# Four units of a retention layer transposed by DMA transfers instead of on TensorE, and the last output tile in two halves

## The chip, the cores and the metric

One NeuronCore of one Trainium2 chip. The metric is the device time of one execution in microseconds (us). Several executions are timed; one of them was also taken by the hardware profiler, and its trace is what the views below show. PE is TensorE (PEld its weight loads), DVE is VectorE, ACT ScalarE, POOL GpSimd, SP SyncE; SPq and ACTq are the parts of SP and ACT that issue DMA transfers.

## The reference

A recurrent retention layer over 4 batches, 8 heads, 768 steps and a head size of 64, followed by a feed-forward network over its 3072 tokens of width 512, with 2048 inner features:

```python
for t in range(S):
    state = gamma[None, :, None, None] * state + np.einsum('bhd,bhe->bhde', k[:, :, t], v[:, :, t])
    y[:, :, t] = scale * np.einsum('bhd,bhde->bhe', q[:, :, t], state)
...
x = attn_out.transpose(0, 2, 1, 3).reshape(B * S, H * D)
h = x @ w_in
g = np.maximum(h, 0.0) + alpha * np.minimum(h, 0.0)
out = g @ w_out
```

Inputs and output are float32; the kernel's matmuls take float16.

## The kernel before, in words

The recurrence is cut into chunks of 128 steps. A *unit* is two neighbouring chunks (256 steps) of four heads; there are 24 units, and four of them (512 tokens, all heads) make one of six *blocks*, on which the feed-forward network runs. The work on unit i:

- `load` (line 110) brings k, q and v of the unit, 256 KB each, on SP's queue, into tiles of a pool of 24 buffers that they share with the float32 pieces of w_out.
- `u_scale(i, 0)` multiplies k by its decay factors, on DVE, or on POOL where it is told so; `u_scale(i, 1)` does q on POOL (line 136). Both write one half of the tile kdq. `u_cast` (line 146) casts v to float16 (tile vx), on POOL (line 152) or ScalarE (line 150).
- kdq has to be transposed into the tile kq. `u_turn` (line 160) does it with eight PE transposes into PSUM (tile trb, line 166) and a copy on ScalarE (line 175). `u_flip` (line 154) does it with one DMA transfer that transposes, on SP's queue (line 156).
- `u_state` (tile stp, line 195) and `u_scores` (tiles sca and scb, line 236) are PE work; the scores read kq. DVE then masks the scores (line 249) and adds to the running state (lines 214, 218), and POOL decays it (line 219). `u_visit` (line 529) puts the state and the scores of one unit together.
- `u_out` (line 259 and after) multiplies masked scores with v and the carried state with q on PE (tile yps, lines 286 and 271), and ScalarE copies the result into xT (line 306), the input of the feed-forward network.

For each block n, `ffn1(n)` makes 16 groups of four matmuls (tile hps, line 326), each followed by a step on ScalarE (line 336) and one on DVE (gt, line 337); `ffn2(n)` multiplies gt with w_out, 64 matmuls into four PSUM tiles (tile ops, line 367), each copied by ScalarE (line 376) and stored. Both are generators: `tick(gen, m)` emits the next m matmuls, and the program writes work on the units between ticks, so that PE gets it between matmuls of the feed-forward network.

The order on every engine is the order of the program's text. Units 0 to 3 come first (0 to 22 us), with `u_turn`. Then `ffn1(0)` and `ffn2(0)` run; in `ffn2(0)` the work on units 4 to 7 is emitted, with `u_turn` as well. For blocks from 2 on, units are prepared on POOL and transposed by `u_flip` in `ffn1(n)`, and visited in `ffn2(n)`.

`ffn2(0)` runs in four parts (`parts=4`): all four output tiles first take w_out pieces 0 to 3, then 4 to 7 and so on, since the pieces are still being loaded and cast (`cast_wo`, on POOL at line 437 or on ScalarE at line 433). SP's queue, in its order: the loads of units 0 to 3, then w_out pieces 0 to 3, unit 4, pieces 4 to 7, unit 5, pieces 8 to 11, unit 6, pieces 12 to 15, unit 7, then units 8 to 11, four output stores, and from then on one `u_flip` ahead of each unit's loads. A transfer that has to wait for a semaphore holds up all that stand behind it on its queue. The transfers use eight completion semaphores in turn, and each waits for the one that had its semaphore before.

Of the kernel before, what the change touches and what calls it, by code (L numbers as in the profile page):

```python
# [9 lines left out]
FP = mybir.dt.float32  # L10
F16 = mybir.dt.float16
COPY = mybir.ActivationFunctionType.Copy
# [6 lines left out]
def kernel(  # L19
# [10 lines left out]
    nc = tc.nc  # L30
    B, H, S, D = q.shape
    d_model, d_ff = moe_w_in.shape
    NFT = d_ff // 128
# [4 lines left out]
    UB = 4  # L38
    NBLK = NU // UB
    TB = UB * C  # L40
    scale = 1.0 / np.sqrt(D)
# [30 lines left out]
    sbp = ctx.enter_context(tc.tile_pool(name="sbp", bufs=1, space=bass.MemoryType.SB))  # L72
# [13 lines left out]
    w_out_all = sbp.tile([128, NFT, d_model], F16, tag="wout", name="wout")  # L86
# [6 lines left out]
    def ps(name, dt=FP, n=512):  # L93
        return psp.tile([128, n], dt, tag="ps", bufs=8, name=name)
# [15 lines left out]
    def load(u, names="kqv"):  # L110
        t = staged.setdefault(u, {})
        for nm in names:
            src = srcs[nm]
            st = sbp.tile([128, H * D], FP, tag="ld", bufs=24, name=f"{nm}s{u}")
            j, g = divmod(u, 2)
            b, c = divmod(2 * j, NCH)
            t[nm] = st
            ins = nc.sync.dma_start(  # L118
                out=st.rearrange("p (h x) -> p h x", h=H // 2),
                in_=src[  # L120
                    b, H // 2 * g : H // 2 * g + H // 2, C * c : C * c + 2 * C, :
                ].rearrange("h (p s) d -> p h (s d)", s=2),
            )
# [4 lines left out]
    def u_scale(i, a, eng=None):  # L128
        if i not in prepped:
            kdq = sbp.tile([128, 2, 2, H // 2, D], F16, tag="kdq", bufs=8, name=f"kdq{i}")  # L130
            kq = sbp.tile([128, 2 * NP, 128], F16, tag="kq", bufs=8, name=f"kq{i}")
            vx = sbp.tile([128, H // 2, 2, D], F16, tag="vx", bufs=8, name=f"vx{i}")
            prepped[i] = (kdq, kq, vx)
        g = i % 2
        o = 2 * H * a
        (eng or (nc.vector, nc.gpsimd)[a]).tensor_tensor(  # L136
            out=prepped[i][0][:, a],
            in0=staged[i]["kq"[a]].rearrange("p (h s d) -> p s h d", s=2, d=D),
            in1=tab[:, o : o + 2 * H]
            .rearrange("p (s h) -> p s h", s=2)[:, :, H // 2 * g : H // 2 * g + H // 2]  # L140
            .unsqueeze(3)
            .to_broadcast([128, 2, H // 2, D]),
            op=MULT,
        )

    def u_cast(i, on_scalar=False):
        o = prepped[i][2].rearrange("p h s d -> p (h s d)")
        x = staged[i]["v"]
        if on_scalar:
            nc.scalar.activation(out=o, in_=x, func=COPY, bias=0.0, scale=1.0)  # L150
        else:
            nc.gpsimd.tensor_copy(out=o, in_=x)  # L152

    def u_flip(i):
        kdu, kq, vx = prepped[i]
        nc.sync.dma_start_transpose(
            out=kq, in_=kdu.rearrange("p a s h d -> p (a s h d)")
        )

    def u_turn(i, parts):  # L160
        kdu, kq, vx = prepped[i]
        trb = ps("trb", F16, 1024)
        for a in parts:
            for x in range(NP):
                c0 = 128 * (NP * a + x)
                nc.tensor.transpose(  # L166
                    out=trb[:, c0 : c0 + 128],
                    in_=kdu[:, a, x // 2, 2 * (x % 2) : 2 * (x % 2) + 2, :].rearrange(
                        "p a d -> p (a d)"
                    ),  # L170
                    identity=ident,
                )
        c0 = 512 * parts[0]
        c1 = 512 * parts[-1] + 512
        nc.scalar.activation(  # L175
            out=kq.rearrange("p a i -> p (a i)")[:, c0:c1],
            in_=trb[:, c0:c1],
            func=COPY,
            bias=0.0,
            scale=1.0,  # L180
        )
# [176 lines left out]
    def ffn2(n, parts=1, late=None):  # L358
        gt = gts.pop(n)
        opss = {}  # L360
        step = NFT // parts
        for f0 in range(0, NFT, step):
            for tq in range(UB):
                if f0 == 0:
                    opss[tq] = ps("ops")
                for ft in range(f0, f0 + step):
                    nc.tensor.matmul(  # L367
                        out=opss[tq],
                        lhsT=gt[:, ft, 128 * tq : 128 * tq + 128],
                        rhs=w_out_all[:, ft, :],  # L370
                        start=(ft == 0),
                        stop=(ft == NFT - 1),
                    )
                    if ft == NFT - 1:
                        os_sb = sbp.tile([128, d_model], FP, tag="os", bufs=6, name="os")
                        nc.scalar.activation(  # L376
                            out=os_sb, in_=opss[tq], func=COPY, bias=0.0, scale=1.0
                        )
                        row = TB * n + 128 * tq
                        if late is None:  # L380
                            nc.scalar.dma_start(out=out[row : row + 128, :], in_=os_sb)
                        else:
                            late.append((row, os_sb))
                    yield

    def tick(gen, m):
        for _ in range(m):
            if next(gen, 1) == 1:
                return
# [11 lines left out]
    for lh in range(2):  # L401
        z = slice(64 * lh, 64 * lh + 64)
        nc.gpsimd.tensor_copy(
            out=gmat[z, :, z],
            in_=tab[z, 4 * H : 4 * H + NP].unsqueeze(2).to_broadcast([64, NP, 64]),
# [9 lines left out]
    def hold(ins):  # L415
        if held:
            tc.add_manual_dep(
                ins.ins,
                held.pop().ins.name,
                mybir.DependencyInfo(  # L420
                    mybir.DependencyClass.Sync, mybir.DependencyReason.DATA
                ),
                reason="loads behind the pieces of w_in",
            )

    def load_wo(i):
        for ft in range(4 * i, 4 * i + 4):
            pieces[ft] = sbp.tile([128, d_model], FP, tag="ld", bufs=24, name=f"wo{ft}")
            hold(nc.sync.dma_start(out=pieces[ft], in_=moe_w_out[128 * ft : 128 * ft + 128, :]))

    def cast_wo(ft, on_scalar=False):
        if on_scalar:
            nc.scalar.activation(
                out=w_out_all[:, ft, :], in_=pieces.pop(ft), func=COPY, bias=0.0, scale=1.0
            )
        else:
            nc.gpsimd.tensor_copy(out=w_out_all[:, ft, :], in_=pieces.pop(ft))  # L437
# [4 lines left out]
    def masked(i):  # L442
        m[i](0)
        m[i](1)
# [53 lines left out]
    st[2](1)  # L498
    m[3](1)
    st[3](1)  # L500
    for i in range(UB):
        load_wo(i)
        load(UB + i)
    gen = ffn1(0, early=4)
    tick(gen, 8)
    u_out(2)
# [2 lines left out]
        out=aps[:, 0:NFT], in_=alpha_sb, identity=tab[0:NFT, NTAB - 16 : NTAB]  # L509
    )  # L510
    nc.vector.tensor_scalar(
        out=oma_sb, in0=aps[:, 0:NFT], scalar1=-1.0, scalar2=1.0, op0=MULT, op1=ADD
# [6 lines left out]
    u_cast(4)  # L519
    for ft in range(4, 8):  # L520
        cast_wo(ft)
    tick(gen, 52)
    u_scale(4, 0)
    for _ in gen:
        pass
    stores = []
    gen = ffn2(0, parts=4, late=stores)

    def u_visit(i):
        st[i] = u_state(i)  # L530
        m[i] = u_scores(i)
        st[i](0)
        masked(i)
        st[i](1)

    def u_prep(i, eng=None):
        u_scale(i, 0, eng)
        u_scale(i, 1)
        u_cast(i)

    tick(gen, 4)
    u_turn(4, (0, 1))
    tick(gen, 6)
    u_visit(4)
    u_prep(5)
    cast_wo(8)
    cast_wo(10)
    tick(gen, 10)
    u_out(4)
    tick(gen, 2)  # L550
    u_turn(5, (0, 1))
    cast_wo(9, True)
    cast_wo(11, True)
    tick(gen, 6)
    u_visit(5)
    u_prep(6)
    cast_wo(12)
    cast_wo(14)
    tick(gen, 8)
    u_out(5)  # L560
    tick(gen, 2)
    u_turn(6, (0, 1))
    cast_wo(13, True)
    cast_wo(15, True)
    u_scale(7, 1)
    u_cast(7)
    tick(gen, 6)
    u_visit(6)
    u_scale(7, 0)
    tick(gen, 8)  # L570
    u_out(6)
    tick(gen, 2)
    u_turn(7, (0, 1))
    tick(gen, 6)
    u_visit(7)
    for _ in gen:
# [5 lines left out]
    gen = ffn1(1, early=4)  # L582
# [3 lines left out]
    for n in range(1, NBLK):  # L586
        more = n + 1 < NBLK
        u0 = UB * (n + 1)
        if n > 1:
            gen = ffn1(n)  # L590
# [9 lines left out]
        gen = ffn2(n)  # L600
# [41 lines left out]
```

## Time and profile before

| | us |
|---|---|
| median of 3 runs (lowest, highest) | 217.64 (216.75, 220.69) |
| the profiled execution | 217.12 |
| its span, first to last instruction | 215.3 |
| units 0 to 3, until the first matmul of ffn1(0) | 0 to 17.4 |
| ffn1(0) | 17.4 to 33.6 |
| ffn2(0), with units 4 to 7 | 33.6 to 53.8 |
| last matmul ends | 211.5 |

A line of the chain of work, or of the timeline, has the start in us, the duration in us (of a merged group: from its first start to its last end, or its share of the chain), the engine, the tiles, the line of the kernel and the number of instructions. Some lines end in brackets with the idle time of the engine ahead of the instruction and what ended it. For a tile, three numbers such as 2.7/4.2/6.4 are minimum, median and maximum. The granted clock of PE is 0.998 of full speed in this execution.

### The profile page before, as it was taken

How to read it: one execution, taken by the hardware profiler on the slowest of the kernel's cores; microseconds unless marked ns; L12 is line 12 of the kernel's file. 1: busy time of each engine (PE TensorE's matmuls, PEld its weight loads, DVE VectorE, ACT ScalarE, POOL GpSimd, SP SyncE). 2: the span in 40 equal slices, each digit the busy share in tenths (PEclk: the TensorE clock that was granted, in tenths of full speed). 3: DMA queues.
4: the chain of work that ended last, by engine and by line, in shares of the span. 5: the costliest groups of instructions: out<-in, count | busy, mean ns of one | idle time of the engine just before them, and what ended most of it. 6: DMA issues, size and time to landing. Idle time of an engine off the chain costs nothing.

```text
span 215.3 us, 5025 instructions
## 1 busy us (share of the span) xinstructions
PE 207.2 (96%) x2053; PEld 105.4 (49%) x2053; DVE 120.6 (56%) x195; ACT 102.9 (48%) x189; POOL 87.0 (40%) x114
## 2 busy tenths in 40 slices
PE   7897999999999999999999999999999999999992
PEld 3455545555644555444555444555444555444440
DVE  2684697455398633488733488533488633488000
ACT  2582874556586223566223576223675223575121
POOL 3485084691891426930145960214950421000000
PEclk9999999999999999999999999999999999999999
DMA  6999999999699911899311799411840111100121
GB/s 168 317 223 200 279 368 373 369 336 331 222 208 313 277 61 49 221 242 307 110 52 52 194 241 298 148 53 49 139 108 0 49 52 52 49 0 2 52 81 65
DMA packets 62599, 36.11 MB, mean 168 GB/s; under 512 B 18912, under 2 KB 57456, under 8 KB 62576
## 3 DMA queue, kind: packets, MB, share of 16 engines
q1 hardware_dynamic: 57792, 28.32, 48.5%
q10 hardware_dynamic: 3200, 5.38, 6.9%
q0 software_dynamic: 1584, 2.10, 5.8%
q8 instruction: 16, 0.26, 0.5%
q14 instruction: 7, 0.06, 0.1%
HBM read 27.40 MB, written 6.29 MB: 156 GB/s over the span
## 4 chain that ended last, share of the span: by engine, by line
PE 89%; DMA 6%; SPq 2%; ACT 1%; POOL 0%; issue 0%
PE ops L367 40%; PE hps L326 39%; PE yps L286 4%; DMA win<-in_moe_w_in_dram 3%; DMA qs<-in_q_dram 3%; PE stp L195 2%; PE yps L271 2%; PE sca L236 2%; SPq L118 2%; PE trb L166 1%; ACT xT L306 1%; PE scb L236 1%; POOL kdq L136 0%; ACT os L376 0%
## 5 line engine op out<-in xcount | busy, mean ns | idle before, releaser
L337 DVE SCALAR_TENSOR_TENSOR gt<-hm,oma,hps 128x512 f16<-128x512 f32 x96 | 69.5, 746 | 35.6 <-ACT hm L336 28.4
L367 PE MATMUL ops<-wout,gt 128*128 128x512 f16 x384 | 89.2, 380 | 0.0
L326 PE MATMUL hps<-xT,win 128*128 128x512 f16 (+1 forms) x416 | 84.8, 363 | 1.2 <-ACT xT L306 0.7
L336 ACT ACTIVATE hm<-hps 128x512 f32<-128x512 f32 x96 | 56.6, 597 | 24.2 <-PE hps L326 23.6
L326 PEld LDWEIGHTS <-win 128*128 128x128 f16 x416 | 40.4, 98 | 43.8 <-issue 1.0
L219 POOL TENSOR_TENSOR tg<-ss,gmat 128x256 f16<-128x256 f32 x32 | 23.5, 735 | 78.2 <-DVE ss L218 72.7
L367 PEld LDWEIGHTS <-gt 128*128 128x128 f16 x384 | 35.3, 98 | 40.2
L306 ACT ACTIVATE xT<-yps 128x256 f16<-128x256 f32 x48 | 18.4, 453 | 40.8 <-PE yps L286 29.0
L376 ACT ACTIVATE os<-ops 128x512 f32<-128x512 f32 x24 | 14.2, 597 | 35.7 <-PE ops L367 35.7
L136 POOL TENSOR_TENSOR kdq<-qs,tab 128x512 f16<-128x512 f32 x24 | 25.0, 1044 | 5.4 <-DMA qs<-in_q_dram 5.4
L218 DVE TENSOR_TENSOR ss<-tg,stp 128x256 f32<-128x256 f16 x32 | 13.2, 416 | 24.3 <-PE stp L195 24.3
L249 DVE TENSOR_TENSOR m<-sca,mi 128x512 f16<-128x512 f32 x24 | 16.4, 685 | 0.8 <-PE sca L236 0.4
L136 POOL TENSOR_TENSOR kdq<-ks,tab 128x512 f16<-128x512 f32 x16 | 16.7, 1044 | 0.0
L249 DVE TENSOR_TENSOR m<-scb,mi 128x512 f16<-128x512 f32 x24 | 16.4, 681 | 0.0
L152 POOL CAST vx<-vs 128x512 f16<-128x512 f32 x20 | 13.2, 658 | 0.0
L175 ACT ACTIVATE kq<-trb 128x512 f16<-128x512 f16 (+1 forms) x11 | 8.7, 790 | 6.2 <-PE trb L166 6.2
L195 PE MATMUL stp<-vx,kdq 64*64 64x128 f16 x320 | 9.7, 219 | 0.7 <-ACT vx L150 0.7
L437 POOL CAST wout<-wo 128x512 f16<-128x512 f32 x12 | 7.5, 651 | 7.0 <-DMA wo<-in_moe_w_out_dram 6.9
L286 PE MATMUL yps<-m,vx 64*64 64x128 f16 x384 | 10.0, 222 | 0.0
L236 PE MATMUL sca<-kq 64*64 64x128 f16 x192 | 9.4, 216 | 0.5 <-ACT kq L175 0.4
L214 DVE TENSOR_TENSOR tg<-stp,gmat 128x256 f16<-128x256 f32 x8 | 3.4, 424 | 11.3 <-PE stp L195 11.3
L236 PE MATMUL scb<-kq 64*64 64x128 f16 x192 | 9.7, 219 | 0.0
(26 smaller groups left out, 73.4 us busy)
## 6 DMA issues: line engine op xcount, KB each, us to landing
ks<-in_k_dram SPq DMA_DIRECT2D x24, 256.0 KB, 4.5
qs<-in_q_dram SPq DMA_DIRECT2D x24, 256.0 KB, 4.7
vs<-in_v_dram SPq DMA_DIRECT2D x24, 256.0 KB, 4.5
out_dram<-os ACTq DMA_DIRECT2D x20, 256.0 KB, 2.0
wo<-in_moe_w_out_dram SPq DMA_DIRECT2D x16, 256.0 KB, 5.2
win<-in_moe_w_in_dram POOLq DMA_DIRECT2D x2, 768.0 KB, 8.8
out_dram<-os SPq DMA_DIRECT2D x4, 256.0 KB, 4.3
win<-in_moe_w_in_dram POOLq DMA_DIRECT2D x1, 512.0 KB, 6.4
```

The lines of the kernel that those rows point to most:

```text
L136: (eng or (nc.vector, nc.gpsimd)[a]).tensor_tensor(out=prepped[i][0][:, a], in0=staged[i]["kq"[a]].rearrange("p (h s d) -> p s h d", s=2, ...
L195: nc.tensor.matmul(out=stps[hf][64 * lh : 64 * lh + 64, 128 * r : 128 * r + 128], lhsT=kdu[z, 0, s, 2 * r + lh, :], rhs=vx[z, 2 * r : 2 * ...
L219: nc.gpsimd.tensor_tensor(out=tgs[u + 1][:, gs, :], in0=new, in1=gmat[:, gs, :], op=MULT)
L236: nc.tensor.matmul(out=scs[lh][z, c0 : c0 + 128], lhsT=kqv[y, 0, s, r, z], rhs=kqv[y, 1, :, r, z], start=True, stop=True,)
L249: nc.vector.tensor_tensor(out=m2, in0=scs[lh].rearrange("p (s r i) -> p s r i", s=2, r=2), in1=masku.unsqueeze(2).to_broadcast([128, 2, 2, ...
L286: nc.tensor.matmul(out=ypss[hf][64 * lh : 64 * lh + 64, 128 * r : 128 * r + 128], lhsT=vx[z, 2 * r + lh, s, :], rhs=m2s[lh][z, s, r, :], s ...
L306: nc.scalar.activation(out=xT[n][:, 2 * g : 2 * g + 2, c0 : c0 + C].rearrange("p a (i s) -> p a s i", s=2), in_=ypss[hf][:, 0:256].rearran ...
L326: nc.tensor.matmul(out=hpss[ft][:, lo:hi], lhsT=w_in_all[:, hp, 128 * ft : 128 * ft + 128], rhs=xT[n][:, hp, lo:hi], start=(hp == 0), stop ...
L336: nc.scalar.activation(out=hm, in_=hpt, func=RELU, bias=0.0, scale=-1.0)
L337: nc.vector.scalar_tensor_tensor(out=gt[:, ft, :], in0=hm, scalar=oma_sb[:, ft : ft + 1], in1=hpt, op0=MULT, op1=ADD,)
L367: nc.tensor.matmul(out=opss[tq], lhsT=gt[:, ft, 128 * tq : 128 * tq + 128], rhs=w_out_all[:, ft, :], start=(ft == 0), stop=(ft == NFT - 1),)
L376: nc.scalar.activation(out=os_sb, in_=opss[tq], func=COPY, bias=0.0, scale=1.0)
```

## The change

Units 4 to 7 are no longer turned on PE: `u_flip` transposes them, placed on SP's queue between the loads, with the v load of the unit that follows behind it. v of units 5, 6 and 7 is cast by ScalarE instead of POOL. The scaling of k and q is emitted earlier, and the visits of units 4 to 7 come after 9, 25, 41 and 57 matmuls of `ffn2(0)` instead of 10, 28, 44 and 60. Of the last output tile of the last block, the left 256 columns are computed, copied and stored first, then the right 256.

```diff
+        def put(tq, lo, hi):
+            os_sb = sbp.tile([128, d_model], FP, tag="os", bufs=6, name="os")
+            nc.scalar.activation(
+                out=os_sb[:, lo:hi], in_=opss[tq][:, lo:hi], func=COPY, bias=0.0, scale=1.0
+            )
...
         for f0 in range(0, NFT, step):
             for tq in range(UB):
...
+                last = n == NBLK - 1 and tq == UB - 1
+                for lo, hi in ((0, 256), (256, 512)) if last else ((0, 512),):
...
+                    for ft in range(f0, f0 + step):
+                        nc.tensor.matmul(
+                            out=opss[tq][:, lo:hi],
+                            lhsT=gt[:, ft, 128 * tq : 128 * tq + 128],
+                            rhs=w_out_all[:, ft, lo:hi],
...
+                        if ft == NFT - 1:
+                            put(tq, lo, hi)
+                        yield
...
-    for i in range(UB):
-        load_wo(i)
-        load(UB + i)
+    load_wo(0)
+    load(4)
+    load_wo(1)
+    load(5, "kq")
     gen = ffn1(0, early=4)
...
-    tick(gen, 52)
+    tick(gen, 40)
     u_scale(4, 0)
+    u_flip(4)
+    load(5, "v")
+    load_wo(2)
+    load(6, "kq")
+    u_scale(5, 1)
     for _ in gen:
         pass
+    u_scale(5, 0)
+    u_flip(5)
+    load(6, "v")
+    load_wo(3)
+    load(7, "kq")
     stores = []
     gen = ffn2(0, parts=4, late=stores)
...
-    tick(gen, 4)
-    u_turn(4, (0, 1))
-    tick(gen, 6)
+    tick(gen, 9)
     u_visit(4)
-    u_prep(5)
+    u_cast(5, on_scalar=True)
+    u_scale(6, 0)
     cast_wo(8)
     cast_wo(10)
+    cast_wo(9, True)
+    cast_wo(11, True)
+    u_scale(6, 1)
+    u_flip(6)
+    load(7, "v")
     tick(gen, 10)
     u_out(4)
-    tick(gen, 2)
-    u_turn(5, (0, 1))
-    cast_wo(9, True)
-    cast_wo(11, True)
     tick(gen, 6)
     u_visit(5)
-    u_prep(6)
+    u_cast(6, on_scalar=True)
+    u_scale(7, 0)
     cast_wo(12)
     cast_wo(14)
-    tick(gen, 8)
+    u_scale(7, 1)
+    u_flip(7)
+    tick(gen, 10)
     u_out(5)
-    tick(gen, 2)
-    u_turn(6, (0, 1))
     cast_wo(13, True)
     cast_wo(15, True)
-    u_scale(7, 1)
-    u_cast(7)
     tick(gen, 6)
+    u_cast(7, on_scalar=True)
     u_visit(6)
-    u_scale(7, 0)
-    tick(gen, 8)
+    tick(gen, 10)
     u_out(6)
-    tick(gen, 2)
-    u_turn(7, (0, 1))
     tick(gen, 6)
     u_visit(7)
```

More of the change, by code (lines that the diff above doesn't have):

```diff
@@ L361, in ffn2 @@
         step = NFT // parts
+        def put(tq, lo, hi):
[3 more added lines that the diff above has]
+            )
+            row = TB * n + 128 * tq
+            if late is None:
+                nc.scalar.dma_start(out=out[row : row + 128, lo:hi], in_=os_sb[:, lo:hi])
+            else:
+                late.append((row, os_sb))
         for f0 in range(0, NFT, step):
             for tq in range(UB):
[L364 to L377, printed above, removed]
-                        )
[L379 to L384, printed above, removed]
+                last = n == NBLK - 1 and tq == UB - 1
+                for lo, hi in ((0, 256), (256, 512)) if last else ((0, 512),):
+                    if f0 == 0:
+                        opss[tq] = ps("ops")
+                    for ft in range(f0, f0 + step):
[3 more added lines that the diff above has]
+                            rhs=w_out_all[:, ft, lo:hi],
+                            start=(ft == 0),
+                            stop=(ft == NFT - 1),
+                        )
+                        if ft == NFT - 1:
+                            put(tq, lo, hi)
+                        yield
     def tick(gen, m):
```

## The prediction

> **What bounds the kernel now.** First the page's first two parts and the chain of work that ended last, then that chain in order of time for the stage that the change touches (33 to 57 us), then what SP's queue issues there and how long each transfer takes to land.
>
> ```profile
> PE 207.2 (96%) x2053; PEld 105.4 (49%) x2053; DVE 120.6 (56%) x195; ACT 102.9 (48%) x189; POOL 87.0 (40%) x114
> ...
> DMA  6999999999699911899311799411840111100121
> ...
> PE 89%; DMA 6%; SPq 2%; ACT 1%; POOL 0%; issue 0%
> ```
>
> PE is busy 96% of the span and is 89% of the chain, so a matmul that goes away shortens the run, unless PE then waits. The DMA row says where it could wait: slices are 5.4 us, and the first ten (to 54 us) are full but the first. After that the DMA engines have air.
>
> ```profile
> 33.61 0.86 PE ops L367 x4
> 34.48 0.45 PE trb L166 x8
> 34.92 1.29 PE ops L367 x6
> 36.22 0.23 PE stp L195 x4
> ...
> 36.78 2.26 PE ops L367 x10
> 39.05 0.35 PE yps L286 x16
> 39.40 0.33 PE yps L271 x4
> ...
> 53.83 0.87 PE hps L326 x8
> ```
>
> This is ffn2 of block 0, 33.61 to 53.83 us, 20.2 us without a hole: 64 ops matmuls (0.216 each), four visits (state and scores, 0.57 each: 36.22 to 36.78), u_out (0.68), and the four groups of eight transposes, 0.45 each. Nothing waits; kq comes from ACT in time.
>
> ```profile
> 28.38 0.38 SPq L118 DMA_DIRECT2D ks<-in_k_dram  x1
> 29.18 0.38 SPq L118 DMA_DIRECT2D qs<-in_q_dram  x1
> 29.91 0.37 SPq L118 DMA_DIRECT2D vs<-in_v_dram  x1
> ```
>
> ```profile
> L156 SPq DMA_TRANSPOSE kq<-kdq x16: 1232/1470/2326, 57.5 to 158.8; - x16
> ```
>
> ```profile
> DMA to landing us min/median/max: 2.7/4.2/6.4
> ```
>
> Those are the loads of unit 5. Each issue on SP waits until the transfer eight places ahead of it has landed (29.18 follows k of unit 4, 23.98 + 5.1 = 29.08; 29.91 follows q of unit 4, 24.49 + 5.4 = 29.89). So the queue always holds eight, and landings set the pace: q of unit 5 lands at 29.18 + 5.6 = 34.78, q of unit 7, 14 loads later, at 39.45 + 5.2 = 44.65: **0.705 us a load**. The second and third fence are the view of tile kq: a transfer that transposes takes 2.7 us to landing when alone and up to 6.4 behind others.
>
> **The change part by part.** *Removed:* four groups of trb, 4 x 0.45 = 1.8 us of PE's unbroken chain. ACT's four copies of kq (1.02 each) go too; ACT waits for PE in this stage, so that is worth nothing by itself.
>
> *Added to SP's queue:* four transposing transfers, each in front of loads that the same stage needs. The order becomes q5, T4, v5, wo8-11, k6, q6, T5, v6, wo12-15, k7, q7, T6, v7, T7, then the loads of units 8 to 11 (T4 is the transpose of unit 4, wo8 piece 8 of w_out). The queue is full, so T5 lands after T4 and seven loads, and T6 after T5 and seven more.
>
> Price of one, from blocks 2 and 3, where one goes in front of three loads. The k loads land at 62.25, 66.24, 69.64, 74.55 and at 90.29, 95.54, 98.87, 102.33 us (issue plus landing). Three loads are 2.12, so the transposes between them cost 1.87, 1.28, 2.79, 2.4 (a store of 0.7 taken off), 1.21 and 1.34. By themselves, from 151 to 161 us, four of them and one store take 7.3 us of all DMA engines, 1.65 each without the store. I take **F = 1.65**, in the middle of the six; ends 1.2 and 2.8. Its own landing comes less far behind the load ahead of it: 1.0, 1.1, 2.6, 0.8, 1.0, 1.2; I take **a = 1.0** (ends 0.8 and 2.6); the rest of F falls on the load behind it. None is zero or below, since each moves bytes on a queue with no air.
>
> [...]
>
> *T4.* It waits for k of unit 4 scaled on DVE and q scaled on POOL. DVE's turn now comes three gt earlier (after 10 of 16), about 29.8 to 30.5; POOL's row is 29.92 + 1.04 = 30.96. So T4 issues at 31.0 instead of v5 at 29.91. Behind the wait stand v5 and wo8-11, but six loads are still in flight until 34.78, which cover the 1.1 us and T4's 1.2 to 2.3 us on SP. T4 lands at 34.78 + 1.0 = 35.8. PE gets to the scores of unit 4 at 33.61 + 9 x 0.216 + 0.23 = 35.8: no stall, none left to spare.
>
> *T5* issues near 36.8 (k scaled on DVE after the last gt, 35.2 plus up to 1.24; q on POOL 34.8 plus 1.04) and lands at 34.78 + 1.65 + 7 x 0.705 + 1.0 = 42.4. PE needs from scores to scores 0.33 + 10 x 0.216 + 0.68 + 6 x 0.216 + 0.23 = 4.7, so it is there at 40.5: **stall 1.9**.
>
> *T6* lands 0.65 + 4.94 + 1.0 = 6.6 after T5, at 49.0. PE (0.12 more for a state of both halves) is there at 42.4 + 4.8 = 47.2: **stall 1.8**.
>
> *T7* waits for q of unit 7 (landed about 48.0) and 1.04 on POOL, so issues at 49.1 and lands by 51.8 to 52; PE is there at 49.0 + 4.8 = 53.8. No stall. Only the loads of units 8 to 11 stand behind that wait.
>
> *v on ScalarE and the casts of w_out.* v5 and v6 land right behind T4 and T5 (37.1, 43.7); a cast is 0.62; the state that reads them comes at 40.3 and 47.1. Pieces 8 to 11 land before T5, 12 to 15 before T6, and the ops that read them come 7 ticks after those scores. On ACT the copies of yps stand behind these casts; the next scores reuse their PSUM tiles, but wait for kq anyway. Nothing.
>
> *Behind the stage.* Four transposes (6.6 us) and about 2 us of an empty queue ahead of T7 push the loads of units 8 to 11 back: the last lands near 62 instead of 55.5 (50.33 + 5.2), T8 issues near 60 instead of 57.46 and lands near 66. Its scores come at 69.5 now and some 2 us later then; the next three transposes follow 3.5 to 4.5 apart, the visits 4.15 apart. Margin 5 us: nothing.
>
> *The last tile in halves.* PE: 32 matmuls of 256 columns at 0.109 (the row of 53.83 above: eight in 0.87, each with its own weights) are 3.49 against 3.46.
>
> ```profile
> 211.51 0.60 ACT L376 ACTIVATE os<-ops 128x512 f32<-128x512 f32 x1 [2.86 <-PE ops L367]
> 212.14 0.34 ACTq L381 DMA_DIRECT2D out_dram<-os  x1
> ```
>
> Only the second half is left after PE's end. Its copy: a 128x256 copy of yps takes 0.45, so 0.15 less than 0.60. Its store: 256 KB land in 2.0, some 0.7 of it data flow (three slices of 0.28 us in the view of the last 11 us), so between 0 and 0.35 less; I take 0.3, as data seem to flow at the rate of the whole. The first half's store goes out 1.7 us earlier and is gone. Together -0.4 (ends -0.1 and -0.5).
>
> *Sum,* against the profiled execution, 217.12 us (span 215.3, 1.8 around it; 0.5 below the median of 217.64): 217.12 - 1.8 + 1.9 + 1.8 - 0.4 = **218.6 us**. The stalls add up to 2 x F + a - 0.64 (the landing of T6, less PE's arrival at the scores of unit 6 without any stall, 35.8 + 4.7 + 4.8). With F = 1.2 and a = 0.8 they are 2.6, and it is 217.5; with F = 2.8 and a = 1.0 they are 6.0, and it is 220.9. The change breaks even at 2 x F + a = 2.8.
>
> **The rivals.**
> 1. *A transpose costs no more than a load* (F = a = 0.705). T5 lands at 41.1, stall 0.6, T6 at 46.8, stall 0.8: 217.12 - 1.8 + 1.4 - 0.4 = **216.4**. [...] For it: the transpose touches no HBM. Against it: the cycles of 3.3 to 4.9 us.
> 2. *Hidden altogether:* the transposes run beside the loads. 217.12 - 1.8 - 0.4 = **214.9**. 2 x F + a would have to be under 0.64. For it: the DMA share in this stage reads 1.11, so packets overlap within an engine. Against: the same cycles.
> 3. *Slower:* place, SP's queue from 31 to 53 us; each transpose costs there what the one of 68.08 us did (F = 2.8, a = 2.6, 6.0 us to landing). T4 then stalls PE 1.6, T5 3.0, T6 2.9: 217.12 + 7.5 - 2.2 = **222.4**. It decides from 2 x F + a = 7.7 on (222.0). For it: eight in flight here, three to four there. Against: two of six cycles only. [...]
> 4. *The stall moves on:* T8 to T11 late for ffn2 of block 1. It needs the 5 us of margin gone; each us beyond costs one: about **220.5**.
>
> **How the numbers follow.** Forecast (217.5 to 220.9) 0.55; rival 1 0.15; rival 2 0.13; rival 3 0.13; rival 4 0.04. The range goes from 215.2 to 221.8: it takes in the forecast's ends, rival 1 and rival 4 and leaves out most of rivals 2 and 3, some 0.2. Two per cent of the median is 4.4 us, about what a measurement of this kernel can tell from no change: faster means under 213.3, which no case gives (0.03 for what I have overlooked); slower means over 222.0, rival 3 (0.13); the rest, 0.84, is the same.
>
> **What would show it.** Right: trb only for units 0 to 3; in the chain, sca or scb released by DMA kq for units 5 and 6, 1 to 3 us each, none for 7; loads of units 8 to 11 landing up to 62 us; T8 near 60; the end 0.4 us closer behind PE's last matmul. Wrong: no PE wait on kq (rival 2), waits under 1 us (rival 1), a wait at unit 4 above 1 us or a granted clock below 1 near 40 us (rival 3), waits on kq after 70 us (rival 4). A PE wait for anything but kq in this stage would mean that I have misread what stands behind a wait on ACT or POOL.

## The result, and the profile after

| | before | after |
|---|---|---|
| median, us (lowest, highest; 4 runs each) | 217.19 (216.54, 220.69) | 223.83 (221.68, 224.21) |
| the profiled execution, us | 217.12 | 221.68 |
| its span, us | 215.3 | 219.9 |
| ffn2(0), first matmul to the first of ffn1(1), us | 33.45 to 53.66: 20.2 | 33.14 to 59.00: 25.9 |
| last matmul to the end of the span, us | 3.8 | 3.0 |

The ratio, of the fast executions alone, is 1.029, with a 95% interval of 1.0245 to 1.0339: slower, and above the range of 215.2 to 221.8 us. The profiled execution is the quickest of the four. The time sits in one place: ffn2(0) takes 5.65 us more (both by the timeline, in which a matmul begins a little earlier than in the chain), and what lies between it and the last matmul takes 157.8 us in both.

The page of after, its first two parts and the chain by engine:

```profile
PE 206.9 (94%) x2037; PEld 105.7 (48%) x2037; DVE 119.9 (55%) x195; ACT 101.0 (46%) x189; POOL 85.3 (39%) x111
...
PEclk9999999996999999999999999999999999999999
DMA  6999999997999981399711399911442012100112
...
PE 75%; DMA 15%; SPq 5%; POOL 2%; ACT 1%; issue 1%
```

PE's work fell by 0.3 us only (the transposes left, the slow clock came), and its share of the chain fell from 89 to 75%: DMA and SP's queue took its place. One slice of the clock row, the tenth (49.5 to 55 us), is below 9. Now the waits of PE on kq, and the chain in order of time for the same stretch:

```profile
PE sca L236 <- DMA kq<-kdq: 5.5, 3, 4.0
```

```profile
43.16 7.89 DMA kq<-kdq
...
51.09 0.31 PE sca L236
...
51.73 3.38 PE ops L381 x10
```

PE waited three times for a transposing transfer, 5.5 us in all, once 4.0. The ten ops matmuls behind that wait take 3.38 us; ten in a row took 2.26 before (at 36.78 us). The three waits are these lines of PE's timeline, with the idle time in brackets:

```profile
35.76 0.24 PE L236 MATMUL sca<-kq 64*64 64x128 f16 x1 [0.18 <-DMA kq<-kdq]
```

```profile
42.05 0.24 PE L236 MATMUL sca<-kq 64*64 64x128 f16 x1 [1.30 <-DMA kq<-kdq]
```

```profile
51.09 0.31 PE L236 MATMUL sca<-kq 64*64 64x128 f16 x1 [4.04 <-DMA kq<-kdq]
```

The first matmul of the third line takes 0.31 us, those of the others 0.24: the clock is already down. The granted clock stands in the table of windows (after each engine's busy time: clock, DMA share, GB/s):

```profile
48.00:50.00 2.00, 0.00 (x0) 0.00 (x0) 0.73 (x2) 0.00 (x0) 1.04 (x1) 1.00 0.89 207
50.00:51.00 1.00, 0.00 (x0) 0.00 (x0) 0.00 (x0) 0.00 (x0) 0.00 (x0) 0.78 0.14 29
51.00:52.00 1.00, 0.91 (x17) 0.53 (x18) 0.22 (x1) 0.43 (x1) 0.00 (x0) 0.50 1.12 248
...
53.00:54.00 1.00, 1.00 (x4) 0.38 (x3) 0.39 (x2) 0.00 (x0) 0.44 (x1) 0.52 1.10 309
54.00:55.00 1.00, 1.00 (x5) 0.29 (x3) 0.00 (x0) 0.00 (x0) 0.29 (x1) 1.00 1.00 249
```

While PE waits the clock goes to 0.50, and it stays there for about 3 us of work. In 50 to 51 us the DMA engines are almost idle too (0.14), though T6 has not landed yet. SP's queue, its transposes of this stage and the next:

```profile
30.82 1.72 SPq L156 DMA_TRANSPOSE kq<-kdq  x1
36.72 2.71 SPq L156 DMA_TRANSPOSE kq<-kdq  x1
43.16 3.81 SPq L156 DMA_TRANSPOSE kq<-kdq  x1
49.70 1.23 SPq L156 DMA_TRANSPOSE kq<-kdq  x1
63.31 1.53 SPq L156 DMA_TRANSPOSE kq<-kdq  x1
```

They land at 35.72, 42.02, 51.06 and 52.50 us, so they take 4.9, 5.3, 7.9 and 2.8. T6 lands 2.5 us behind the load ahead of it (q7, 48.55).

The data of T6 had moved long before that. The page of after counts 4240 packets under 512 bytes more than that of before, 1060 for each of the four transposing transfers. From 46.20 to 49.03 us 1077 such packets start; in the next 1.8 us, 49.05 to 50.85, there are 17:

```profile
DMA packets 365, 0.19 MB, mean 103 GB/s; under 512 B 17, under 2 KB 364, under 8 KB 364
```

At 48.7 to 48.8 us, ahead of the last of them, the view has one packet that isn't the kernel's data, 16 KB of instructions. It takes 69.5% of 16 engines in 0.1 us, which is as much as one engine does in 1.1 us:

```profile
q8 instruction: 1, 0.02, 69.5%
```

T4, T5 and T7 land 0.5 to 0.6 us behind their last packet, T6 2.0. Four traces have T6 behind the same seven loads. In after, in its second run and in the kernel with `keep(14)` below, the packet of instructions starts 0.2 to 0.3 us ahead of T6's last one, and T6 lands 2.0 us behind its last packet and 8.7 to 9.0 behind T5. In the price experiment below it starts at 53.74, when T6 has landed (53.62): 0.6 us behind the last packet, 7.3 behind T5. No run moved the instructions by themselves, so that they hold up the landing is argued from these traces, not shown.

*The sum of the trace.* Transposes gone -1.8; waits +5.5; the slow clock +1.4 (the ten ops 3.38 - 2.26 = 1.1, the scores ahead of them 0.64 - 0.33 = 0.3); some 0.5 more at the three waits, where state and scores take about 0.75 us without the wait and the slow clock, against 0.57 before: together the stage's 5.65. The end comes 0.8 closer to the last matmul, and ffn2(0) starts 0.3 earlier. 217.12 + 5.65 - 0.8 - 0.3 gives 221.7 against 221.68.

### The profile page after: what moved, and what is told of

It reads as the page before. It is cut to its first block, busy times and chain, and to the rows that moved or that the text cites. A ratio compares the mean times of both kernels' runs of the same rounds, so it can differ in the third digit from the quotient of the medians.

```text
span 219.9 us, 4977 instructions
## 1 busy us (share of the span) xinstructions
PE 206.9 (94%) x2037; PEld 105.7 (48%) x2037; DVE 119.9 (55%) x195; ACT 101.0 (46%) x189; POOL 85.3 (39%) x111
## 4 chain that ended last, share of the span: by engine, by line
PE 75%; DMA 15%; SPq 5%; POOL 2%; ACT 1%; issue 1%
PE ops L381 35%; PE hps L326 31%; DMA qs<-in_q_dram 4%; DMA win<-in_moe_w_in_dram 4%; DMA kq<-kdq 4%; SPq L118 3%; PE yps L286 3%; DMA wo<-in_moe_w_out_dram 3%; PE stp L195 2%; SPq L435 2%; PE sca L236 2%; PE yps L271 2%; POOL kdq L136 1%; ACT xT L306 1%; POOL wout L443 1%
## 5 line engine op out<-in xcount | busy, mean ns | idle before, releaser
L381 PE MATMUL ops<-wout,gt 128*128 128x512 f16 (+1 forms) x400 | 89.7, 374 | 0.0
L381 PEld LDWEIGHTS <-gt 128*128 128x128 f16 x400 | 37.4, 99 | 40.7 <-issue 1.7
L365 ACT ACTIVATE os<-ops 128x512 f32<-128x512 f32 (+1 forms) x25 | 14.5, 580 | 34.2 <-PE ops L381 34.1
L136 POOL TENSOR_TENSOR kdq<-qs,tab 128x512 f16<-128x512 f32 x24 | 26.0, 1082 | 8.9 <-DMA qs<-in_q_dram 8.7
L218 DVE TENSOR_TENSOR ss<-tg,stp 128x256 f32<-128x256 f16 x32 | 13.2, 416 | 20.3 <-PE stp L195 20.3
L136 DVE TENSOR_TENSOR kdq<-ks,tab 128x512 f16<-128x512 f32 x8 | 6.0, 754 | 10.4 <-DMA ks<-in_k_dram 10.4
L236 PEld LDWEIGHTS <-kq 64*64 64x64 f16 x384 | 7.7, 108 | 7.5 <-DMA kq<-kdq 6.0
L152 POOL CAST vx<-vs 128x512 f16<-128x512 f32 x17 | 10.9, 639 | 0.0
```

The source lines that it names most:

```text
L136: (eng or (nc.vector, nc.gpsimd)[a]).tensor_tensor(out=prepped[i][0][:, a], in0=staged[i]["kq"[a]].rearrange("p (h s d) -> p s h d", s=2, ...
L236: nc.tensor.matmul(out=scs[lh][z, c0 : c0 + 128], lhsT=kqv[y, 0, s, r, z], rhs=kqv[y, 1, :, r, z], start=True, stop=True,)
L365: nc.scalar.activation(out=os_sb[:, lo:hi], in_=opss[tq][:, lo:hi], func=COPY, bias=0.0, scale=1.0)
L381: nc.tensor.matmul(out=opss[tq][:, lo:hi], lhsT=gt[:, ft, 128 * tq : 128 * tq + 128], rhs=w_out_all[:, ft, lo:hi], start=(ft == 0), stop=( ...
```

## The experiments

My theory: the price of a transposing transfer in this full queue was set too low, and the wait that came of it was long enough to take the clock down. Rivals: something else in the change (ScalarE's casts, the visits' places, the halves) makes the loss; T6 is late because seven loads stand ahead of it in one queue, whatever the transfer itself costs.

**All units on PE again, the rest of the change kept**

```diff
-    u_flip(4)
...
-    tick(gen, 9)
+    tick(gen, 3)
+    u_turn(4, (0, 1))
+    tick(gen, 6)
```

Units 5 to 7 likewise, each turned six matmuls ahead of its visit.

> The changed kernel, but units 4 to 7 are transposed on PE again (six ops matmuls ahead of each visit); casts, order of loads, place of the visits and the halves of the last tile stay. Theory (the loss is PE waiting for kq, which queues behind seven loads on SP): no wait on DMA kq in ffn2(0), granted clock 1.00 there, stage of about 20.2 us, and the end 0.8 us closer: 216.0 to 217.0 us. Rival (v on ScalarE, the casts of w_out on ScalarE ahead of the copies of yps, or the place of the visits cost the time): stays above 219.

216.84 against 217.25 us, ratio 0.9965 (0.992 to 1.001). The stage takes 20.9 us, no wait on a transfer is left in it, and the clock reads 1.00. The transfers are the whole loss; the other parts of the change cost nothing that can be seen but 0.4 us of wait for ACT's copy at unit 5 and some 0.2 around it.

**PE kept busy ahead of the scores of unit 6**

```diff
+    keep(14)
     u_visit(6)
```

`keep(14)` emits 14 matmuls of 512 columns that nobody reads.

> The changed kernel with 14 matmuls on constant data (3.0 us, result unused) ahead of the visit of unit 6, inside the 4.0 us in which PE waits for kq. Theory (an idle PE loses its clock, and that costs time of its own): the scores of unit 6 start at the same 51 us, but the granted clock stays 1.00 behind them; about 1.5 us less than the changed kernel. Rival (the ten slow ops matmuls of 0.34 us are slow for another reason, such as the transfers): the same time as the changed kernel, within 0.3 us.

222.5 us, ratio 1.0235 (1.0145 to 1.0324). The interval overlaps that of after, so the times settle nothing; the trace does. (As a whole that execution is no faster, 223.89 us: its ffn2(0) starts 3 us later than after's.) PE's timeline there:

```profile
50.14 3.19 PE L100 MATMUL kps<-spin 128*128 128x512 f16 x14
...
54.62 0.24 PE L236 MATMUL sca<-kq 64*64 64x128 f16 x1 [0.95 <-DMA kq<-kdq]
54.97 2.33 PE L381 MATMUL ops<-wout,gt 128*128 128x512 f16 x10
```

and after, the same ten matmuls:

```profile
51.67 3.45 PE L381 MATMUL ops<-wout,gt 128*128 128x512 f16 x10
```

With PE busy until shortly before kq lands, the ten take 2.33 us instead of 3.45. T6 was no earlier for it (it landed 8.97 us behind T5, 9.04 in after), so what went away is the clock's share. From the landing of T6 to the state of unit 7 it is 4.54 us here, 5.85 in after, and 7.26 in a second run of after below: the clock cost 1.3 to 2.7 us.

**The halves of the last tile alone** (before with the new `ffn2`, twice)

```diff
-                for ft in range(f0, f0 + step):
+                for lo, hi in ((0, 256), (256, 512)) if last else ((0, 512),):
+                    for ft in range(f0, f0 + step):
```

> The kernel before with nothing but the last output tile in two halves. Prediction on record: 0.4 us less than before (0.1 to 0.5). The trace of the changed kernel, from PE's last matmul to the end of the span, 3.03 against 3.81 us: 0.8 less. Rival: 32 matmuls of 256 columns cost more than 16 of 512 and eat it: no gain.

> Once more the kernel before with the last output tile in halves, in more rounds: in five traces so far the end of the span lies 3.0 to 3.3 us behind PE's last matmul, against 3.81 in the one trace of before, so 0.5 to 0.8 us less, ratio 0.996 to 0.998. Rival: what the timed runs gave, 1.0023 (0.9985 to 1.0061), no gain at all.

217.52 us, ratio 1.0023 (0.9985 to 1.0061), and 216.82 us, 0.9999 (0.9962 to 1.0035). In the traces the last matmul is 3.34 and 3.31 us before the end, 0.5 less than in before; the times don't resolve it. The half's copy in after, whose bracket shows that it waits for PE alone:

```profile
216.89 0.38 ACT L365 ACTIVATE os<-ops 128x256 f32<-128x256 f32 x1 [1.36 <-PE ops L381]
```

It takes 0.38 us, 0.22 less than the copy of the whole tile.

**Transposes further forward in the queue**: T5 ahead of k6 and q6, T6 ahead of two pieces of w_out and of k7 and q7.

```diff
-    load(6, "kq")
...
     u_flip(5)
-    load(6, "v")
-    load_wo(3)
-    load(7, "kq")
+    load(6)
+    load_wo(3, 0, 2)
...
     u_flip(6)
-    load(7, "v")
+    load_wo(3, 2, 4)
+    load(7)
```

> The changed kernel with two transposes further to the front of SP's queue: that of unit 5 ahead of k and q of unit 6 (two loads fewer before it), that of unit 6 ahead of w_out pieces 14 and 15 and of k and q of unit 7 (four fewer). Theory (kq waits for what stands before it on the queue): kq of unit 5 lands 1.4 us earlier, about 40.6, that of unit 6 at 46 to 48 instead of 51; the stall at unit 6 falls under 3 us and the clock stays 1.00: 2 to 4 us less than the changed kernel, 218 to 220. Rival (a transpose is slow by itself in this stage, wherever it stands): kq of unit 6 still 7 to 9 us behind kq of unit 5, same time as the changed kernel.

221.23 us, ratio 1.0151 (1.0057 to 1.0244): half of the loss is gone, but the time stays above the 218 to 220 expected. PE's waits:

```profile
PE sca L236 <- DMA kq<-kdq: 2.9, 3, 1.4
PE yps L286 <- DVE m L249: 2.2, 3, 1.7
```

No wait is long and the clock reads 1.00. But moving the loads back makes k7 late (50.86 us, 47.68 in after); DVE waits for it to scale it, the masks of unit 6 stand behind that on DVE, and PE waits for the masks. T6's data were through at 46.14, but it landed at 48.15, again 2.0 us later, with a packet of instructions at 45.98. In this stage the order in the queue chose who was late.

**The price by itself**: transfers that nobody reads, near the end of the kernel: six transposes, eight loads of k, then twice a transpose and seven loads of k, and twice a transpose and seven pieces of w_out.

```diff
+        for _ in range(6):
+            turn()
+        for _ in range(8):
+            fetch(False)
+        for _ in range(2):
+            turn()
+            for _ in range(7):
+                fetch(False)
...
+        if not more:
+            price()
```

> The changed kernel with 42 extra transfers on SP's queue behind the last transpose, where the DMA engines have little else to do: six transposes of kdq of unit 23 into spare tiles, eight loads of k (rows of 512 bytes), then twice one transpose and seven such loads, then twice one transpose and seven pieces of w_out (rows of 2 KB). None is read. The landings give the price of a transpose by itself, F, behind seven loads of either kind. Theory of the prediction: 1.65 us each, alone or in front of loads, its own landing 1.0 behind the load ahead of it. Rival (what the changed kernel's trace suggests): 1.2 to 1.7 alone, but 2.2 to 2.6 in a full queue of loads. The run's total time means nothing here, beyond that it ends with the last of them or with the last store.

SP's issues of the six together:

```profile
167.30 8.02 SPq L603 DMA_TRANSPOSE xkq<-kdq  x6
```

Back to back, one lands every 1.36 us (171.45 to 176.86 for four steps), at the pace at which SP issues them. In front of loads, from the first load of one cycle to that of the next: 7.69 and 9.16 us with loads of k, 6.21 with pieces of w_out. Taking off the seven loads at the interval they keep there (0.72; 0.61), 2.7, 4.1 and 1.9 are left. But an output store of ACT lands in each of the three (at 191.2, 201.1 and 208.7); with 0.7 for it, as in the prediction, a transpose costs 2.0, 3.4 and 1.2. The second cycle also has a packet of instructions in it (198.67). The DMA engines' share and GB/s, first with transposes alone:

```profile
167.00:169.00 2.00, 2.00 (x11) 0.90 (x10) 1.77 (x3) 1.45 (x3) 0.00 (x0) 1.00 0.92 179
169.00:171.00 2.00, 2.00 (x11) 0.94 (x10) 1.76 (x3) 1.47 (x3) 0.00 (x0) 1.00 0.89 200
171.00:173.00 2.00, 2.00 (x40) 0.99 (x38) 1.66 (x3) 1.27 (x3) 0.00 (x0) 1.00 0.81 184
```

and in before, with loads alone:

```profile
35.00:40.00 5.00, 5.00 (x63) 2.44 (x62) 2.93 (x5) 1.33 (x3) 2.83 (x4) 1.00 1.10 371
```

At four fifths of that share the transposes move half as much. A transpose so takes about 0.87 x 1.36 = 1.2 us of all sixteen engines, a load 1.10 x 0.705 = 0.8. In a full queue it cost that (1.2) or more. Theory (1.65) and rival (2.2 to 2.6) aren't told apart by three cycles so far apart.

**Two units flipped, two on PE**: 4 and 7 by transfers, 5 and 6 on PE.

```diff
-    u_flip(5)
...
-    u_flip(6)
...
+    u_turn(5, (0, 1))
...
+    u_turn(6, (0, 1))
```

> Only units 4 and 7 are transposed on SP's queue, units 5 and 6 on PE; the visit of unit 4 two ops matmuls later; w_out casts behind the copy of kq on ScalarE; halves of the last tile stay. Theory (only T5 and T6 stand behind seven loads each and come late): no wait of PE on DMA kq above 0.3 us, granted clock 1.00, two groups of transposes less (0.9 us): 215.5 to 216.8. Rival (each transpose on this queue costs PE about 2 us, wherever it stands): 219 or more.

217.09 us, ratio 0.9975 (0.9938 to 1.0012), the same as before and not the 215.5 to 216.8 of the theory. T7, issued at 48.68 with the queue empty, lands at 51.48 and no one waits; T4 lands at 37.00 and costs 1.0 us, about what two groups of trb gave (0.9).

**The transposes of 5, 6 and 7 on ACT's queue**, 4 on PE, SP's loads without a hole.

```diff
-    def u_flip(i):
+    def u_flip(i, eng=None):
...
-        nc.sync.dma_start_transpose(
+        (eng or nc.sync).dma_start_transpose(
...
+    u_flip(5, nc.scalar)
```

> Unit 4 is transposed on PE; the transposes of units 5 to 7 are issued from ACT's queue instead of SP's, SP's queue holds only loads. Theory (a transpose is late because it stands behind seven loads in one queue): from ACT's queue each lands 3 to 4.5 us after its issue although the DMA engines are as busy; no stall at units 5 to 7 above 1 us: 215.5 to 217.5. Rival (the DMA engines are what is short, whichever queue): 5 to 8 us from issue to landing as on SP, stalls of 1 us and more each, 219 or more; or ACT, held up while it issues, makes PE wait for its copies.

223.54 us, ratio 1.0293 (1.0233 to 1.0353): as slow as after. The issues (38.84, 42.35 and 50.26 us), and the wait on PE:

```profile
L156 ACTq DMA_TRANSPOSE kq<-kdq x3: 1248/1257/1317, 38.8 to 50.3; - x3
```

```profile
46.49 0.31 PE L236 MATMUL sca<-kq 64*64 64x128 f16 x1 [5.19 <-DMA kq<-kdq]
```

They land at 46.4, 50.15 and 57.6 us, 7.3 to 7.8 after their issue, though nothing stands ahead of them in their queue; loads on SP take up to 8.6. That a transpose is late because it stands behind seven loads in one queue falls. That all queues together hold more work than the DMA engines do in time fits, and the kernel with half of the w_out loads below bears it out.

**After once more**

> The changed kernel once more, as the measure for the others on this chip, and a second trace: kq of unit 6 should land 8.5 to 9.5 us behind kq of unit 5 again, PE's wait for it be 3 to 4.5 us, and the clock fall once behind it; 221.5 to 224.5 us. If that wait is under 2 us here, the first trace was a freak.

224.81 us, ratio 1.035 (1.0277 to 1.0423), a little above the 224.5 expected. The profile shows another share of the same loss:

```profile
38.51 0.31 PE L236 MATMUL sca<-kq 64*64 64x128 f16 x1 [3.08 <-DMA kq<-kdq]
```

```profile
52.85 0.31 PE L236 MATMUL sca<-kq 64*64 64x128 f16 x1 [3.02 <-DMA kq<-kdq]
53.43 4.45 PE L381 MATMUL ops<-wout,gt 128*128 128x512 f16 x10
```

T4 was late here (38.46; k5 ahead of it took 7.1 us), T5 was not waited for, T6 landed 8.69 behind T5. Both waits are 3 us, and the matmuls behind both are slow, where one fall of the clock was expected: the ten behind them took 3.64 and 4.45 (mean granted clock of the execution: 0.976). The stage is 29.2 us long.

**Half of the loads of w_out left out**: pieces 8 to 15 are zeros written by POOL, so the second half of the last product is left out.

```diff
+        if ft >= 8:
+            nc.gpsimd.memset(w_out_all[:, ft, :], 0.0)
+            return
...
-    load_wo(2)
...
-    load_wo(3)
```

> The changed kernel without the loads of w_out pieces 8 to 15: their half of w_out is filled with zeros on POOL instead, so the second half of the last product is left out. Eight of the 20 loads from unit 5 to unit 7 are gone, T5 and T6 stand behind three loads each. Theory (transposes are late because the DMA engines are short in this stage, not because of the queue, SP or the waits for POOL and DVE): kq lands 3 to 5 us after each issue, PE's waits on kq add up to under 1 us, clock 1.00, and with 1.8 us of transposes and 0.6 of the tail gone it is 214.5 to 216.0. Rival (the chain q landed, scaled, transposed is too long by itself): waits of 2 us and more remain, 218 or above.

216.91 us, ratio 0.9961 (0.9917 to 1.0005), above the 214.5 to 216.0 of the theory. T4, still in the full queue, takes 6.3 us and costs PE 1.9; T5, T6 and T7 land 3.3, 4.0 and 4.0 after their issue, and nothing waits for them. With 2 MB fewer to load, PE waited for one of the four transposes only. The casts of those pieces are gone as well, so ScalarE had less to do too; but the waits that went were waits for the transfers.

**Two units flipped, visits later**: the kernel with two flips, with visits after 17, 31, 45 and 59 matmuls (the last edit three times, between a visit and the next u_out).

```diff
-    tick(gen, 11)
+    tick(gen, 17)
...
-    tick(gen, 10)
+    tick(gen, 8)
```

> Units 4 and 7 transposed on SP's queue, 5 and 6 on PE, as in the run with two transposes, but the visits of units 4 to 7 after 17, 31, 45 and 59 ops matmuls instead of 11, 27, 43 and 59, so that kq of unit 4, which came 1.0 us late there, has landed. Theory: no wait on kq at all, ffn2(0) 19.2 to 19.6 us long against 20.2 before, 215.2 to 216.2 us, ratio to before 0.991 to 0.996. Rival: the loads that T4 pushes back (k, q and v of units 5 to 7) come late for the PE transposes instead: no better than before.

216.78 us, ratio 0.9986 (0.9951 to 1.002). The stage is 19.3 us, 0.9 less than before: two groups of trb gone and no wait on kq. Its span is 214.9, before's 215.3; the times don't resolve it, and 216.78 is above the 215.2 to 216.2 expected. A late transpose took part of the gain back behind the stage: the one issued at 69.74 landed at 76.20, an output store and the copies of xT stood behind it on ACT, and PE waited for those:

```profile
76.69 0.76 ACT L306 ACTIVATE xT<-yps 128x256 f16<-128x256 f32 x2 [4.31 <-DMA kq<-kdq]
```

```profile
77.19 0.27 PE L271 MATMUL yps<-kq,tg 128*128 128x128 f16 x2 [1.19 <-ACT xT L306]
```

No kernel here beats before measurably.

## Why the prediction was wrong, point by point

- *Transposes removed, 1.8 us.* Right: trb runs for units 0 to 3 only.
- *T4, 35.8 us, no stall, none to spare.* Right in this execution (35.72, 0.18). "None to spare" is what the other executions show: 1.0 with two flips, 1.9 with the light queue, 3.1 in the second run of after, whenever the loads of unit 5 came late.
- *T5, 42.4 us, stall 1.9.* 42.02 and 1.30. T4 had cost the queue 1.2, 0.4 less than F; in the kernel with `keep(14)` it cost 2.7, so the near hit is partly luck.
- ***T6, 49.0 us, stall 1.8: the step that failed, by the terms F and a.*** It landed at 51.06, and PE waited 4.04. From q5 to T6 the queue took 51.06 - 34.82 = 16.24 us; fourteen loads at 0.705 are 9.87, so 2 x F + a was 6.4, where I had put 4.3. By the landings of q5, q6, q7 and T6 (34.82, 41.00, 48.56, 51.06), less seven loads each, T4 cost 1.2, T5 2.6 and a was 2.5, against 1.65, 1.65 and 1.0. The kernel with `keep(14)` gives 7.7 (37.02 to 54.55), the second run of after 6.1 (36.83 to 52.83). In all three a is 2.5, the largest miss: T6's landing came 2.0 us behind its last packet instead of 0.5 to 0.6, for which the sum had no term. The one cycle in which I had read such an a (2.6, the transpose issued at 68.08) has the same 2.0 us, and a packet of instructions at 72.03; I took it for a dear price and left it at the end of the range. T5's F is 2.3 to 2.6 in all three, T4's 1.2 to 2.7; the price experiment doesn't say more than 1.2 to 3.4. My own upper end, 6.6, held two of the three.
- ***The clock: no term in the sum.*** Even 6.6 made only 220.9. The rest is the clock, which I named as a sign of rival 3 (a granted clock below 1 near 40 us) and left out of the sum, since no wait of PE behind its first matmul was longer than 0.6 us in before. That says nothing of a wait that the change makes. The trace of before has a fall of the clock at its end, where no work is left to slow: PE's last matmul ends at 211.5, and the clock reads 0.67 from 214.5 to 215 us and 0.50 behind that. In this stage a wait of 4.04 us in after, which began at 47.05, brought a clock of 0.50 from 50.6 to 54.0 us, and waits of 3.08 and 3.02 us in its second run were followed by matmuls as slow or slower (ten in 3.64 and 4.45 us); a wait of 2.21 us in the kernel with `keep(14)` was not (ten in 2.33). The length of one wait didn't decide it alone: in the kernel with `keep(14)` a wait of 2.07 us for w_in, which ended at 19.09, was followed by a clock of 0.50 from 20.3 us on, and in the first run of the halves alone one of 1.45 was (mean clocks of the two executions: 0.991 and 0.992). The slow clock cost 1.4 us in the profiled execution, about 4.4 in the second run of after: there -1.8 + 6.1 of waits + 4.4 = 8.7 of the stage's 9.0. The stalls together were about in my range; but 5.5 us of waits with one of 4.04 among them cost 1.4 us more than their length, while in the kernel with the transposes further forward waits of 6 us on kq, masks and xT, the longest 1.7, left the clock at 1.00 (221.23 us).
- *T7, no stall, landed by 52.* Right: 52.50.
- *ScalarE's casts and the visits' places, nothing.* Right, by the first experiment.
- *Behind the stage, nothing.* Right, though sizes were short: the last load of units 8 to 11 landed at 64.80 (62 predicted), T8 was issued at 63.31 (60). PE doesn't wait for kq after 52 us.
- *The last tile, -0.4.* The traces give -0.5 to -0.8; the times show nothing.
- *The rivals.* 1 and 2 needed 2 x F + a at or below 2.1, and fell. No run shows the term of rival 1, a transpose that costs the queue no more than a load (0.705): back to back one lands per 1.36 us, and in this stage F was 1.2 to 2.7. Rival 3 came nearest, with 222.4 us; its place was right, its waits (1.6, 3.0, 2.9) were not those found (0.2, 1.3, 4.0). The chance of 0.13 on it was too small: it asked only for the price that two of six cycles showed. Rival 4 didn't happen.

Open: why T5 cost the queue 2.3 to 2.6 us, when a transpose takes only about 1.2 us of all engines by the estimate from the price experiment, and whether the packet of instructions is what held T6 up. What the landings show is below.

## What to carry to other kernels

Take the price of a transfer from the rows whose queue is as full as the one it goes to, not from the middle of all rows, and find out of a dear row when its data had moved and what else was in the engines then; in this stage, where a load of before landed every 0.705 us, what T4 and T5 cost the queue (1.2 and 2.6 us in after) was paid again by T6, which lands behind both. When a change makes a wait of PE, look at how long the single wait gets: in this stage waits of at most 1.7 us cost their length (the clock stayed at 1.00), one of 4.04 and one of 3.02 us also cost 1.3 and 2.7 us of slow matmuls behind them. Ask of a transfer that replaces engine work what else has to be moved in its stage: for the last three of the four PE waited 5.3 us in after, and not at all once 2 MB less was to be loaded.

## What the runs showed of the hardware that was not expected

- *Some transposes landed 2.0 us behind their last data packet, others 0.5 to 0.6.* It was 2.0 in after, its second run, the kernel with `keep(14)`, the one with the transposes further forward and, at 74.05 us, in before, each time with a 16 KB packet of instructions that starts 0.3 us or less ahead of the last data packet's end. The packet doesn't always come with it: in before one starts at 133.46, 0.3 us ahead of the end of a transpose's data (133.73), which lands 0.6 us behind them (134.34).
- *Landings paused about once for each transpose.* In after the pieces of w_out land 0.7 us apart, but from piece 12 to 13, two transfers behind T5, it is 2.3 us (43.21 to 45.50), and the windows 42 to 46 us still move 323 to 328 GB/s; two loads behind T7 it is 2.05 (55.00 to 57.05). The kernels with other orders have such pauses of 1.8 to 3.5 us as well, and a few came without a transpose near. What makes them was not shown.
- *A queue of its own didn't help:* 7.3 to 7.8 us to landing on ACT's queue, 4.9 to 7.9 behind loads on SP's.
- *A transpose held SP longer with loads ahead of it:* 1.23 us with one load and T6 still to land (T7), 1.72, 2.71 and 3.81 with more loads (T4, T5, T6).
